# Nystromformer attention and a feed-forward layer on one core: batch 1's second layer by seven products, row variances from ScalarE's sums, W1 loaded into memory of W2 and hT

## The chip, the core and the metric

The kernel runs on one core of a Trainium2 chip. The core has five engines that work side by side and wait for each other by semaphores: TensorE (PE in the profile; PEld are its weight loads), VectorE (DVE), ScalarE (ACT), GpSimd (POOL) and SyncE (SP), and 16 DMA engines. The metric is the time of one execution on the device in microseconds.

## What is computed

Eight batches of eight heads, 576 rows, 64 columns. Attention goes through 32 landmarks (means of 18 rows); the inverse of the landmark matrix comes from six steps of an iteration. Its result is normalized by row, goes through two layers (512 to 2048 to 512) with a ReLU between, and is added to what goes in.

```python
def _attn_ref(q, k, v):
    q_lm, k_lm = q.reshape(B, H, 32, 18, D).mean(axis=3), k.reshape(B, H, 32, 18, D).mean(axis=3)
    A, Bm, C = sm(q, k_lm), sm(q_lm, k_lm), sm(q_lm, k)
    ...
    for _ in range(6):
        Z = 2 * Z - Z @ Bm @ Z
    return A @ Z @ C @ v

def _moe_ref(x, g_ln, w_ch1, w_ch2):
    mu = np.mean(x, axis=-1, keepdims=True)
    var = np.mean((x - mu) ** 2, axis=-1, keepdims=True)
    xn = (x - mu) / np.sqrt(var + 1e-06) * g_ln
    return x + np.maximum(xn @ w_ch1, 0.0) @ w_ch2
```

Inputs and outputs are float32; the kernel multiplies in float16.

## The kernel before

The work is cut into some 1,570 steps ("ops") with names; each step issues a few instructions on one engine. `def_...` functions define them, and the text `ORDER` gives the sequence in which they are issued and the letter of the engine that takes each (P TensorE, D VectorE, A ScalarE, G GpSimd, S SyncE). Each engine executes its own steps in that sequence, so the table is a schedule written out by hand or by a planner; buffers are taken from pools of fixed size (`slots`) at the first use and given back after the last, and a step waits on the chip where it uses a buffer that an earlier step still holds.

The batches go through in a staggered pipeline: while PE does the second layer of one batch, the other engines prepare the attention of the next. The steps by batch `b`:

- `load_...`, `cast_...`: q, k and v come in by DMA. Batch 0's q and k go through `stg` buffers, are cast, and are transposed on PE (`turns`, `turned`) and summed to landmarks (`sums`, tiles `pss_q`, `pss_k`). Of later batches GpSimd's queue loads q and k (`nat_q`, `nat_k`) with a cast on the way.
- `warm_i`: matmuls on zeros (tile `idle`) whose result nobody reads: one block of 24 with 160 columns, and 14 blocks of four with 128.
- `psb`, `softmax`, `gram`, `step`, `next`: the landmark matrix (tile `it`) and the iteration, alternating between PE and DVE; then `zt`, `zc`, `zcbd`.
- `load_w1_i`, `scale_w1_ic` (L346 to L360): W1 comes in eight parts of 512 KB into `w1s` tiles, which share the six `stg` buffers with batch 0's q, k and v, and is scaled by `g` into `w1_16`. `load_w2_i`: W2 comes in four parts on GpSimd's queue, cast to float16 into `w2_16`. `less_mean`, `less`, `center` take the mean out of W1.
- `rows_bi`, `x_bi` (`def_rows`): the attention's result `psy` on PE, and its copy to the row blocks `x_j` of 128 rows. Two batches are nine blocks; four belong to the even batch and five to the odd one (`group_of`).
- `measure_j`, `rstd_b` (`def_measure`): mean and variance of each row by VectorE's BN_STATS and BN_AGGR (L997, L998), and the reciprocal of the deviation on ScalarE (a logarithm and an exponential).
- `psm`, `m16`, `psh`, `relu` (`def_first`): the first layer. Each of 16 `psh` tiles takes four matmuls of 288 columns; its ReLU goes to `hT` on ScalarE or VectorE. `psh` tiles, with several others, share two PSUM buffers (`p2`).
- The second layer. For batches 0 and 1 (`b < FAST`), `pso_...` steps multiply block by block: 16 matmuls of 512 columns each (`def_block`), and one addition on VectorE (`done`). From batch 2 on, the first four blocks go by seven products of half-size matrices instead of eight (`def_seven`): sums and differences of parts of hT (`hmix`: eight a batch) and of W2 (`mix_0` to `mix_3`, once for all batches: 16 steps, `def_mixes`), then 16 matmuls of 256 columns a product (tiles `ps7a`, `ps7e`, `ps7c`), and 14 additions of half a block (`add7`). The odd batch's fifth block stays with `pso`. The very last block is done in two parts, `pso_74a` with 384 columns and `pso_74b` with 128.
- `store_...`: the blocks go out by DMA.

Of the kernel before, what the change touches and what calls it, by code (L numbers as in the profile page):

```python
# [11 lines left out]
UINT32 = mybir.dt.uint32  # L12
AF = mybir.ActivationFunctionType
# [6 lines left out]
0G 20P 23P 4S 12P 14P 24P 17P 11P 2S 1S 3S 6S 7S 10P 21P 28G 38P 25A 26D 34P 39D 40P 29P 30A 31P 27D  # L20
37P 32P 42D 41D 18P 33D 43P 65P 44A 45D 66A 61P 67P 46P 47P 250G 48D 22P 19P 15P 62A 68A 69A 71D
245G 49P 50D 63P 35P 13P 79G 80D 51P 52D 64A 36A 81P 70D 53P 72P 73A 5S 95S 54D 8P 9D 105A 106G 55P
56D 57P 74P 82D 260P 83D 58D 16P 84D 96S 59P 75A 76A 60D 85P 251D 86D 89P 90D 87P 88D 126P 261A 262D
108G 77G 94S 103G 93S 97S 101G 91D 92D 78D 107A 102G 127P 128P 129P 130A 167P 141P 142A 252P 253A
145P 169D 104A 168D 98S 254D 149P 150D 147P 148A 172P 173A 176P 247P 177A 248A 259D 255D 174P 175A
246D 256P 257A 146A 170P 171D 109G 110G 121P 122P 123P 111G 124P 268P 156P 258D 151D 249D 267P 112A
125A 275A 269A 270A 271A 157D 277A 158D 131P 132P 133P 134P 178P 163P 278D 279D 117G 273A 433G 274A
99S 113G 135A 180D 263S 164A 159P 280P 281D 160A 165P 166A 114G 264A 100S 115G 116G 265S 118G 136P
137P 266G 161P 179D 429G 119G 138P 139P 162D 282P 283D 140A 181P 182A 183P 284P 276D 285A 143P 187P
184D 286P 144A 188A 272D 152D 185P 186A 287D 297P 298D 299D 189P 191D 190D 288P 289A 294P 290P 295A  # L30
201P 202P 296A 300P 301A 291D 292P 293A 120G 455G 212P 213P 435G 436G 437G 310P 438G 445G 302A 303G
308P 309A 214P 330P 434D 444D 312D 311D 313D 332D 192P 193A 153D 154D 198P 199A 155A 441D 430D 439D
431D 331D 442D 440D 432D 443D 234P 556D 215P 304P 235P 236P 305A 306A 196P 446G 447G 203P 204P 194P
195A 237P 238P 205P 206P 451G 197A 307G 314P 315A 337P 339P 448G 449D 822G 338A 555D 239P 240P 241P
322P 207P 208P 574D 565D 569G 450D 340A 323A 216P 242D 209D 210S 217P 324D 341P 343D 223P 335P 244S
336A 342D 333P 463D 218P 219P 577G 452D 220D 344P 352P 353D 467G 468G 469G 470G 334A 826G 348P 345A
349A 346P 347A 457G 318P 319A 224P 316P 317A 225P 226P 227P 481P 458G 465D 459G 460G 482A 350P 454D
354D 357P 471D 464D 472D 351A 453D 363P 228P 229P 364D 358A 361P 230P 362A 461D 462D 365D 493P 494A
359P 368P 360A 483P 495P 355P 325D 326D 505A 369A 356A 231D 233A 200G 374P 375P 366P 367A 370P 371A
573G 506D 456D 507P 508P 509D 320P 321D 385P 484P 486A 487A 489A 510P 834D 511D 466D 491A 386P 387P  # L40
485A 388P 211S 512P 376P 473S 474G 490A 377P 496P 498A 501A 499A 497A 513D 514P 327D 488D 492D 328D
396P 397P 475S 476G 566G 828G 829G 830G 831G 572G 477S 478G 838G 839G 844G 564G 568G 503A 378P 379P
380P 515D 823D 502A 221S 504D 372P 516P 479S 480A 500D 517D 836D 528P 529P 530D 531D 398P 399P 373A
381P 522P 518P 389P 329A 866S 382D 418P 519D 824D 559D 520P 521D 523A 532P 419P 420P 524A 533A 534A
558D 550P 551D 552D 553D 548P 549A 421P 422P 423P 536P 424P 425P 848G 535G 832D 833D 554D 232S 867A
537A 538A 539G 560D 525P 527A 400P 401P 557D 426D 427S 605P 526A 606A 840G 841G 594P 595A 561D 540P
541A 390P 391P 611P 612A 837D 596D 827D 392P 393D 825D 850G 851G 852G 563D 603P 604A 853G 562D 859D
842D 860G 861G 843D 579P 613P 614A 407P 580A 601P 602A 609P 610A 1217G 585P 408P 845D 599P 409P 607P
600A 410P 411P 586A 597P 608A 542A 543G 856D 615P 598A 576G 626P 616A 412P 413P 581P 627A 402P 862G
394S 582A 570G 567D 617D 589D 835D 863G 858D 590D 618P 619A 634P 635A 643P 583P 584A 620P 621A 624P  # L50
414P 571G 874P 625A 622P 623A 628P 629A 644P 544P 847D 857D 545A 846D 591D 546A 875D 403P 632P 872S
633A 645P 630P 647P 592D 631A 646P 415D 877P 648P 649P 650P 864D 865D 854D 404D 855D 1191G 886P 638D
637G 641G 663P 664P 665P 639D 640D 662G 428S 417S 406S 661D 593A 882A 884A 879A 880A 883A 652D 878A
651D 657D 887A 889P 892A 896A 658D 666P 668D 894A 895A 849D 667D 653P 654P 711P 722P 712A 723A 891A
890A 655P 656P 547G 575G 675P 676P 677P 728P 729A 678P 695P 696A 1192D 713D 716P 881D 1194D 717A
724P 725A 876P 888P 1213G 660D 587P 870S 714P 416S 659D 871G 873G 384S 1229G 642G 1230G 1231G 726P
898A 715A 679D 682D 669P 897D 727A 588A 730P 222S 1232G 899D 900P 901P 731A 718P 732P 902D 743P 719D
578G 903P 904D 670P 720P 734A 733A 721D 744A 671P 672P 673D 699P 700A 893D 739P 636G 1203D 1239S
# [50 lines left out]
def kernel(  # L109
# [61 lines left out]
    def T(name):  # L171
        return handles[name]
# [1091 lines left out]
```

## Time and profile before

| | us |
|---|---|
| runs before (3), median | 260.66 |
| lowest and highest of them | 260.17, 260.79 |
| span of the profiled execution, first to last instruction | 258.5 |
| PE busy | 249.9 |
| DVE busy | 212.3 |
| POOL busy | 177.5 |
| ACT busy | 163.9 |
| matmuls | 3499 |

The profile is of one execution; its span leaves out what lies around the first and the last instruction, so it stands a little below the runs' times. Rows of the groups show the line of the helper that issued the instruction, the engine, the operation, tile written <- tiles read, shapes, the count, the busy time, the mean time of one in ns, and how long the engine sat idle just before them. L193 issues all matmuls of the steps, so these are told apart by their tiles. A matmul's row begins when it is issued and ends with a modelled end, so neighbours overlap.

### The profile page before, as it was taken

How to read it: one execution, taken by the hardware profiler on the slowest of the kernel's cores; microseconds unless marked ns; L12 is line 12 of the kernel's file. 1: busy time of each engine (PE TensorE's matmuls, PEld its weight loads, DVE VectorE, ACT ScalarE, POOL GpSimd, SP SyncE). 2: the span in 40 equal slices, each digit the busy share in tenths (PEclk: the TensorE clock that was granted, in tenths of full speed). 3: DMA queues.
4: the chain of work that ended last, by engine and by line, in shares of the span. 5: the costliest groups of instructions: out<-in, count | busy, mean ns of one | idle time of the engine just before them, and what ended most of it. 6: DMA issues, size and time to landing. Idle time of an engine off the chain costs nothing.

```text
span 258.5 us, 8351 instructions
## 1 busy us (share of the span) xinstructions
PE 249.9 (97%) x3499; PEld 179.8 (70%) x3499; DVE 212.3 (82%) x472; ACT 163.9 (63%) x304; POOL 177.5 (69%) x180
## 2 busy tenths in 40 slices
PE   7898999999999999999999999999999999999993
PEld 7766465556554557777766787777867787788981
DVE  1669899999999989997998869898547999878661
ACT  1588886747766999778756997868666245644000
POOL 8324899689794789699999995782078505966600
PEclk9999999999999999999999999999999999999999
DMA  6999999999749176949704832500130100510356
GB/s 234 367 269 338 374 210 208 207 235 244 227 127 178 29 164 87 221 89 286 140 4 121 231 93 61 127 3 3 41 85 0 44 20 9 115 23 20 82 121 184
DMA packets 23277, 36.32 MB, mean 140 GB/s; under 512 B 2116, under 2 KB 11592, under 8 KB 23240
## 3 DMA queue, kind: packets, MB, share of 16 engines
q1 hardware_dynamic: 12456, 23.37, 29.6%
q0 software_dynamic: 9504, 10.36, 25.1%
q10 hardware_dynamic: 1280, 2.07, 3.1%
q8 instruction: 27, 0.44, 0.7%
q14 instruction: 10, 0.08, 0.1%
HBM read 36.70 MB, written 9.44 MB: 178 GB/s over the span
## 4 chain that ended last, share of the span: by engine, by line
PE 85%; DMA 7%; ACT 3%; DVE 2%; issue 1%; SPq 1%; ACTq 0%; DVEq 0%
PE psh L193 23%; PE ps7a L193 16%; PE pso L193 15%; PE ps7c L193 8%; DMA w1s<-in_moe_w_ch_dram 5%; PE ps7e L193 4%; PE psm L193 3%; PE psy L193 3%; DMA stg_q<-in_q_dram 3%; PE it L193 2%; PE pscv L193 2%; PE psd L193 1%; PE psec L193 1%; PE psea L193 1%; PE pso_74a L193 1%
## 5 line engine op out<-in xcount | busy, mean ns | idle before, releaser
L203 ACT ACTIVATE hT<-psh 128x576 f16<-128x576 f32 x106 | 65.8, 650 | 30.4 <-PE psh L193 28.6
L193 PEld LDWEIGHTS <-hT 128*128 128x128 f16 x688 | 64.6, 98 | 22.6 <-issue 3.1
L193 PE MATMUL psh<-ea,m 128*128 128x288 f16 x512 | 78.2, 286 | 0.1
L193 PEld LDWEIGHTS <-m 128*128 128x128 f16 x512 | 48.9, 98 | 15.6 <-issue 1.3
L193 PE MATMUL pso<-w,hT 128*128 128x512 f16 x176 | 45.5, 380 | 0.0
L207 POOL TENSOR_TENSOR mix<-hT 128x1024 f16<-128x1024 f16 x8 | 17.0, 2125 | 27.4 <-ACT hT L203 27.4
L210 DVE SCALAR_TENSOR_TENSOR x<-ps7a,rstd,x 128x256 f32<-128x256 f32 x48 | 21.3, 477 | 6.7 <-PE ps7a L193 4.9
L193 PE MATMUL ps7a<-mix,hT 128*128 128x256 f16 x192 | 25.9, 273 | 0.0
L1068 DVE TENSOR_SCALAR hT<-psh 128x576 f16<-128x576 f32 x22 | 16.4, 753 | 10.1 <-PE psh L193 9.9
L997 DVE BATCH_NORM_STATS2 six<-x 128x6 f32<-128x512 f32 x36 | 24.2, 673 | 0.0
L207 POOL TENSOR_TENSOR ea<-ea,lns 128x576 f16<-128x576 f16 (+1 forms) x14 | 17.7, 1261 | 7.2 <-ACT lns L203 4.0
L200 ACT CAST m<-psm 128x512 f16<-128x512 f32 (+1 forms) x25 | 19.1, 793 | 4.5 <-PE psm L193 3.4
L200 ACT COPY x<-psy 128x512 f32<-128x512 f32 (+1 forms) x29 | 16.8, 587 | 7.6 <-PE psy L193 7.2
L193 PEld LDWEIGHTS <-mix 128*128 128x128 f16 x192 | 18.2, 98 | 4.3 <-issue 1.5
L207 POOL TENSOR_TENSOR mix<-mix,hT 128x1024 f16<-128x1024 f16 x8 | 16.9, 2124 | 6.2 <-DVE mix L207 5.8
L207 POOL TENSOR_TENSOR hT<-hT 128x1024 f16<-128x1024 f16 x9 | 19.1, 2123 | 0.2
L207 POOL TENSOR_TENSOR hT<-hT,mix 128x1024 f16<-128x1024 f16 x7 | 15.1, 2166 | 4.4 <-PE ps7e L193 2.5
L214 DVE TENSOR_REDUCE part<-xT_k 128x32 f16<-128x576 f16 x24 | 17.1, 737 | 0.0
L207 POOL TENSOR_TENSOR asum_q<-asum_q 128x256 f32<-128x256 f32 (+1 forms) x24 | 15.1, 628 | 1.5
L203 ACT ACTIVATE ec<-psec 128x256 f16<-128x256 f32 (+1 forms) x42 | 12.4, 428 | 5.3 <-PE psec L193 5.3
L193 PE MATMUL psy<-zcbd,ea 128*128 128x256 f16 x80 | 14.8, 273 | 0.2 <-ACT x L200 0.2
L200 POOL CAST natv<-stg_v 128x1152 f16<-128x1152 f32 (+1 forms) x12 | 13.8, 1163 | 1.4 <-DMA stg_v<-in_v_dram 1.3
(174 smaller groups left out, 471.2 us busy)
## 6 DMA issues: line engine op xcount, KB each, us to landing
out_dram<-x SPq DMA_DIRECT2D x55, 128.0 KB, 2.7
stg_v<-in_v_dram SPq DMA_DIRECT2D x10, 576.0 KB, 5.1
w1s<-in_moe_w_ch_dram SPq DMA_DIRECT2D x8, 512.0 KB, 11.6
nat_q<-in_q_dram POOLq DMA_DIRECT2D x7, 576.0 KB, 8.7
nat_k<-in_k_dram POOLq DMA_DIRECT2D x7, 576.0 KB, 7.5
w<-in_moe_w_ch_dram POOLq DMA_DIRECT2D x4, 512.0 KB, 8.5
out_dram<-x ACTq DMA_DIRECT2D x15, 128.0 KB, 2.4
stg_v<-in_v_dram SPq DMA_DIRECT2D x6, 288.0 KB, 4.5
```

The costliest lines, as they stand in the source:

```text
L193: keep(nc.tensor.matmul(o, l, r, start=start, stop=stop, tile_position=(rb, cb), skip_group_check=(skip or cb != 0)))
L200: keep(nc.scalar.copy(o, i) if e == "A" else ENGINES[e].tensor_copy(out=o, in_=i))
L203: keep(nc.scalar.activation(*args, **kw))
L207: keep(ENGINES[e].tensor_tensor(out=o, in0=a, in1=b, op=f))
L210: keep(ENGINES[e].scalar_tensor_tensor(out=o, in0=a, scalar=s, in1=b, op0=f0, op1=f1))
L214: keep(nc.vector.tensor_reduce(out=o, in_=i, axis=axis, op=f))
L997: keep(nc.vector.bn_stats(out=T(f"six_{j}")[:], in_=T(f"x_{j}")[:]))
L1068: keep(nc.vector.tensor_scalar(out=o, in0=T(psh)[:, :, 0:HS], scalar1=0.0, scalar2=None, op0=ALU.max))
```

## The change

Five edits, and a new `ORDER`:

1. `FAST` goes from 2 to 1: batch 1's first four blocks take the seven products. Its 64 `pso` matmuls and four additions go, and 112 matmuls of 256 columns, eight `hmix` steps and 14 half additions come; the W2 mixes are wanted from batch 1 on.
2. For batches 0 to 2 (`BY_SUMS`) the copy of `psy` to `x` also gives the row's sum. The variance then comes from one ScalarE instruction, a Square of (sum - 512 x) with its sum over the row, in place of BN_STATS and BN_AGGR. In the list all 13 measures of these batches go to ScalarE; Of the 14 copies with a sum 11 stand on ScalarE and three on VectorE, there as a TENSOR_SCALAR.
3. W1's parts 0 to 3 are loaded into the memory of `w2_16` and parts 4 to 7 into that of batch 1's `hT`, so that they need no `stg` buffer; W2's loads and batch 1's hT then wait until those parts are scaled.
4. Pools: `s16` has three buffers where it had four.
5. The list: five relus go from VectorE to ScalarE, five W2 mixes and one hT mix more stand on VectorE, seven hT mixes more and five W2 mixes fewer on GpSimd, besides smaller exchanges.

```diff
 ORDER = """
-0G 20P 23P 4S 12P 14P 24P 17P 11P 2S 1S 3S 6S 7S 10P 21P 28G 38P 25A 26D 34P 39D 40P 29P 30A 31P 27D
...
+0G 15P 17P 13P 22P 12P 19P 16P 11P 14P 21P 2S 26A 18P 20P 23P 250G 24P 32P 33A 1S 34P 25D 29P 31P
...
-    FAST = 2
+    FAST = 1
+    BY_SUMS = (0, 1, 2)
...
+    def copy_summed(e, o, i, total):
+        if e == "A":
+            act(o, i, AF.Copy, accum_out=total)
+        else:
+            keep(nc.vector.tensor_scalar(out=o, in0=i, scalar1=1.0, scalar2=0.0, op0=ALU.mult, op1=ALU.add,
+                                         accum_out=total))
...
-                    ("part", 2), ("tot", 3), ("lmt", 4), ("s16", 4), ("sT", 1),
+                    ("part", 2), ("tot", 3), ("lmt", 4), ("s16", 3), ("sT", 1),
...
+        def place_of(i):
+            f, half = divmod(i, 2)
+            if f < 2:
+                return w2_16[:, ts(i, 4), :].rearrange("p m d -> p (m d)").bitcast(FP32).rearrange(
+                    "p (c d) -> p c d", c=2)
+            return T(hT(1))[:].rearrange("p m t -> p (m t)")[:, ts(i - 4, 4 * DM)].bitcast(FP32).rearrange(
+                "p (c d) -> p c d", c=2)
...
-            n = f"w1s_{i}"
-            buf(n, "stg", [P, 2, DM], FP32)
             f, half = divmod(i, 2)
-            op(f"load_w1_{i}", "S", (n,),
-               lambda e, n=n, f=f, half=half: dma(
-                   e, T(n)[:], w1_src[:, 2 * half:2 * half + 2, ts(f, DM)]))
+            op(f"load_w1_{i}", "S", held(i),
+               lambda e, i=i, f=f, half=half: dma(e, place_of(i), w1_src[:, 2 * half:2 * half + 2, ts(f, DM)]))
...
+                st, six = T(f"stats_{b}")[:, u, :], T(f"six_{j}")
+                if e == "A":
+                    act(squares[:], T(f"x_{j}")[:], AF.Square, bias=st[:, 0:1], scale=-float(DM), accum_out=st[:, 1:2])
+                    return
...
-            act(T(f"lnv_{b}")[:, 0:n], T(f"stats_{b}")[:, 0:n, 1], AF.Ln, bias=eps_ln[:], scale=UP * UP)
+            act(T(f"lnv_{b}")[:, 0:n], T(f"stats_{b}")[:, 0:n, 1], AF.Ln, bias=eps_ln[:],
+                scale=UP * UP / DM ** 3 if summed else UP * UP)
```

How the list moves instructions, at three places.

TensorE's queue at the start (`idle` are the blocks on zeros, here the one of 24 with 160 columns; `pst_k`, `pst_q` are batch 0's transposes, `pss_k`, `pss_q` its sums), before:

```order
L193 MATMUL idle_247<-zeros_63 128x160
L193 LDWEIGHTS zeros_63
L193 MATMUL idle_272<-zeros_63 128x128
...
L193 MATMUL idle_272<-zeros_63 128x128
L197 LDWEIGHTS nat_k_277
L197 MATMUL pst_k_279<-ident16_64,nat_k_277 128x128
```

and now:

```order
L196 MATMUL pss_q_313<-pm16_67,nat_q_301 128x64
L196 LDWEIGHTS zeros_63
L196 MATMUL idle_323<-zeros_63 128x160
...
L196 MATMUL idle_323<-zeros_63 128x160
L196 LDWEIGHTS nat_k_253
L196 MATMUL pss_k_291<-pm16_67,nat_k_253 128x64
```

The block of 24, which was the eighth block of all, stands behind the first sums of q and ahead of k's second sums and transposes; all 14 blocks of four stand ahead of the first transposes, where six stood behind them. On SyncE's queue all eight parts of W1 now stand ahead of batch 1's v, where one stood behind half of it, in the order 2, 3, 0, 5, 1, 4, 6, 7 (before 2, 3, 1, 0, 4, 5, 6, 7).

ScalarE's queue between the exponentials of batches 2 and 3 (`ec`, from `psec`) and batch 1's deviation (`lnv`), before:

```order
L203 ACTIVATE ec_1782<-psec_1747 128x2x2x32
L203 ACTIVATE ec_1782<-psec_1747 128x4x2x32
L200 CAST natv1_77<-stg_v_1878 128x2x9x64
L203 ACTIVATE hT_1334<-psh_1857 128x576
L203 ACTIVATE lnv_2026<-stats_1368,eps_ln_73 128x5
```

and now (`squares` is written by a Square and read by nobody; its sum goes to `stats`):

```order
L206 ACTIVATE squares_75,stats_731<-x_1542,stats_731 128x512
L206 ACTIVATE x_1774,stats_731<-psy_1614 128x512
L206 ACTIVATE ec_1716<-psec_1679 128x4x2x32
L206 ACTIVATE hT_743<-psh_1765 128x576
L206 ACTIVATE ec_1716<-psec_1679 128x4x2x32
L203 CAST natv1_78<-stg_v_1734 128x2x9x64
L206 ACTIVATE squares_75,stats_731<-x_1533,stats_731 128x512
L206 ACTIVATE squares_75,stats_731<-x_1774,stats_731 128x512
L206 ACTIVATE lnv_1934<-stats_731,eps_ln_73 128x5
```

Three Squares and a copy with a sum have come in among the exponentials and the last relu of batch 1.

VectorE's queue at the very end (the last block's two parts, and ahead of them the last half additions), before:

```order
L210 SCALAR_TENSOR_TENSOR x_4938<-ps7c_5378,rstd_5299,x_4938 128x256
L210 SCALAR_TENSOR_TENSOR x_5211<-ps7a_5219,rstd_5299,x_5211 128x256
L210 SCALAR_TENSOR_TENSOR x_5206<-ps7a_5219,rstd_5299,x_5206 128x256
L210 SCALAR_TENSOR_TENSOR x_5267<-pso_74b_5394,rstd_5299,x_5267 128x128
L210 SCALAR_TENSOR_TENSOR x_5267<-pso_74a_5497,rstd_5299,x_5267 128x384
```

and now:

```order
L220 SCALAR_TENSOR_TENSOR x_5158<-ps7c_5414,rstd_5392,x_5158 128x256
L220 SCALAR_TENSOR_TENSOR x_5368<-ps7a_5383,rstd_5392,x_5368 128x256
L220 SCALAR_TENSOR_TENSOR x_5262<-ps7a_5383,rstd_5392,x_5262 128x256
L220 SCALAR_TENSOR_TENSOR x_5095<-pso_74a_5459,rstd_5392,x_5095 128x384
L220 SCALAR_TENSOR_TENSOR x_5095<-pso_74b_5543,rstd_5392,x_5095 128x128
```

The two parts have changed places, on PE as on VectorE: the 16 matmuls of the small part are now PE's last.

210 lines of the change are left out of this document (115 added, 95 removed).

## The prediction

> **What bounds the kernel now.** I read the busy shares first, then the windows, then the chain of work that ended last, and last the groups that the change touches.
>
> ```profile
> span 258.5 us, 8351 instructions
> PE 249.9 (97%) x3499; PEld 179.8 (70%) x3499; DVE 212.3 (82%) x472; ACT 163.9 (63%) x304; POOL 177.5 (69%) x180
> PE 85%; DMA 7%; ACT 3%; DVE 2%; issue 1%; SPq 1%; ACTq 0%; DVEq 0%
> ```
>
> TensorE is busy for 97% of the span, and 85% of the chain lies on it; the 7% on DMAs is the start. A busy PE need not be at its peak, so I look at how fast it goes where it carries the chain (start us, length us, what).
>
> ```profile
> 52.08 1.73 PE pso L193 x8
> 98.61 0.98 PE psh L193 x8
> 245.87 1.75 PE ps7a L193 x16
> ```
>
> A product of 512 columns takes 1.73 / 8 = 0.216 us, one of 288 columns 0.1225, one of 256 columns 1.75 / 16 = 0.109: time goes with the columns, from 52 us to 246 us alike. So between the start and the end a product that is left out is time saved, as long as the others come no later. The windows say where that holds (stretch, length, then PE, PEld, DVE, ACT, POOL busy, clock, DMA share, GB/s).
>
> ```profile
> 0.00:10.00 10.00, 8.16 (x101) 7.99 (x101) 3.18 (x11) 2.60 (x3) 6.29 (x29) 1.00 0.80 292
> 10.00:20.00 10.00, 8.70 (x247) 6.58 (x245) 7.17 (x25) 8.13 (x14) 2.85 (x4) 1.00 1.11 286
> 20.00:30.00 10.00, 9.35 (x127) 5.59 (x126) 8.93 (x22) 7.94 (x21) 6.66 (x10) 1.00 1.07 365
> 30.00:40.00 10.00, 9.67 (x145) 6.21 (x145) 9.63 (x26) 8.20 (x17) 9.18 (x13) 1.00 1.19 240
> 50.00:60.00 10.00, 10.00 (x73) 5.46 (x72) 9.95 (x20) 5.83 (x11) 7.74 (x10) 1.00 1.13 248
> 90.00:100.00 10.00, 10.00 (x82) 6.35 (x81) 9.08 (x18) 9.51 (x17) 9.06 (x12) 1.00 0.74 145
> ```
>
> From 40 us on PE has no free time that a window shows, while VectorE is nearly as full up to 130 us. Before 40 us PE is free for 1.30 + 0.65 + 0.33 = 2.3 us of the last three of these first windows, and the DMA engines are full (shares over 1). The chain says what PE waits for there, and what comes at the end:
>
> ```profile
> 15.84 11.95 DMA w1s<-in_moe_w_ch_dram
> 27.81 0.73 ACT w L203
> 252.53 1.64 PE pso_74a L193 x10
> 254.19 0.62 DVE x L210
> ```
>
> **Term 1, batch 1's second layer: -1.6 us.** Four of batch 1's five blocks go from 16 products of 512 columns each (64) to seven half-size products of 16 matmuls of 256 columns each (112). Removed: 64 x 0.216 = 13.84 us. Added: 112 x 0.109375 = 12.25 us. All of it stands on PE between about 60 and 90 us, where PE is full, so the difference counts whole: -1.59 us. Two waits come with it. The products wait for the four mixes of W2, which are wanted a batch earlier, and for eight mixes of hT; behind a waiting product the whole of PE's queue stands still. I take 0, since two of the seven products need no mix and stand first, and name a late mix as the price: up to 2.1 us, once.
>
> **Term 2, the end: -0.3 us.** The last block is stored in two parts. Before, PE ends with the part of 384 columns, whose addition takes 0.62 us; now it ends with the part of 128 columns (0.35 us), and the larger addition runs beside the small part's 16 matmuls.
>
> ```profile
> 252.57 0.35 DVE L210 SCALAR_TENSOR_TENSOR x<-pso_74b,rstd,x 128x128 f32<-128x128 f32 x1 [0.43 <-PE pso_74b L193]
> out_dram<-x SPq DMA_DIRECT2D x1, 96.0 KB, 2.1
> out_dram<-x ACTq DMA_DIRECT2D x1, 96.0 KB, 2.4
> out_dram<-x SPq DMA_DIRECT2D x2, 32.0 KB, 2.7
> ```
>
> That is 0.35 - 0.62 = -0.27 us. The last store is then 32 KB where it was 96 KB; the landings (2.1 to 2.7 us) don't order by size, so I count nothing for it; by these rows it lies between -0.3 and +0.6 us.
>
> **Term 3, the other engines: 0 us.** These are the groups (busy us, mean ns of one):
>
> ```profile
> L997 DVE BATCH_NORM_STATS2 six<-x 128x6 f32<-128x512 f32 x36 | 24.2, 673 | 0.0
> L998 DVE BATCH_NORM_AGGREGATE stats<-six 128x2 f32<-128x6 f32 x36 | 6.6, 182 | 1.2
> L210 DVE SCALAR_TENSOR_TENSOR x<-ps7a,rstd,x 128x256 f32<-128x256 f32 x48 | 21.3, 477 | 6.7 <-PE ps7a L193 4.9 <-ACT rstd L203 0.9 <-PE psh L193 0.6
> L210 DVE SCALAR_TENSOR_TENSOR x<-pso,rstd,x 128x512 f32<-128x512 f32 x11 | 8.0, 731 | 0.4 <-PE pso L193 0.4
> L203 ACT ACTIVATE w<-w1s,g_sb 128x512 f16<-128x512 f32 x4 | 2.9, 720 | 0.9 <-DMA w1s<-in_moe_w_ch_dram 0.9
> L200 ACT COPY x<-psy 128x512 f32<-128x512 f32 x24 | 13.9, 588 | 6.7 <-PE psy L193 6.4
> L207 POOL TENSOR_TENSOR hT<-hT 128x1024 f16<-128x1024 f16 x9 | 19.1, 2123 | 0.2
> L207 POOL TENSOR_TENSOR mix<-w 128x512 f16<-128x512 f16 x5 | 5.8, 1156 | 0.0
> L207 DVE TENSOR_TENSOR mix<-w 128x512 f16<-128x512 f16 x3 | 1.3, 452 | 0.0
> L203 ACT ACTIVATE hT<-psh 128x576 f16<-128x576 f32 x106 | 65.8, 650 | 30.4 <-PE psh L193 28.6 <-DVE mix L207 0.8
> L1068 DVE TENSOR_SCALAR hT<-psh 128x576 f16<-128x576 f32 x22 | 16.4, 753 | 10.1 <-PE psh L193 9.9
> ```
>
> VectorE loses 13 measures (13 x 0.855 = 11.1 us), four whole additions (2.9) and five relus (3.8); it gains 14 half additions (6.7), five mixes of W2 (2.3) and a mix of hT (0.8): about -8 us. ScalarE gains 13 Squares and five relus (3.3). No row shows a Square; the nearest is the scaling of W1, 128x512 from SBUF with an operand per partition, at 0.72 us: 9.4 us, +13 us in all. The sums that it now gives beside copies and Squares have no row; I bound them by nothing and by the 0.13 us that the scaling stands above the plain copy (24 or so times, 3 us), and take nothing. GpSimd gains seven mixes of hT (14.9) and loses five of W2 (5.8): +9 us. So DVE would stand at 204, ACT at 177, POOL at 187 of some 257 us. A Square also waits for its row's sum, which mostly ScalarE itself has just given. All three engines stay below PE, so this work is hidden; if that cover failed, one Square is 0.72 us and one mix 2.1 us of waiting.
>
> **Term 4, the start: 0 us, between -2.3 and +1.6 us.** W1 no longer waits for `stg` buffers, but the DMA engines are full from 10 to 40 us, and the bytes ahead of W1's sixth part (k, q, v, five parts) are the same; what PE waits for at 27.8 us therefore lands when it did. GpSimd's two loads of batch 1's q and k, which share the DMA engines with W1, move too, q's ahead of a cast and k's behind one; their bytes are the same, and I count 0. If W1 came earlier, PE could win its free time there, 2.3 us. Against that, the block of 24 idle matmuls is moved from ahead of the first transposes to behind the first half's sums. Twelve idle matmuls of 128 columns end in 0.84 us (below), so 24 of 160 columns take 24 x 0.07 to 0.09 us = 1.7 to 2.1 us, and k's and q's second halves queue behind them: sums that started at 10.24 us start at up to 11.8, so up to +1.6 us for the iteration of batch 0. That delay ends in the wait for W1, which I take to hide it. W2's loads now wait until W1's first four parts are scaled out of its memory, and GpSimd's scalings of the last parts and loads of the next q and k are queued behind them; they stood behind those scalings on GpSimd's queue already, and the DMA engines are full for long after (share 1.13 in 50 to 60 us): 0, at most one scaling, 0.7 us.
>
> ```profile
> 1.40 6.26 PE L193 MATMUL idle<-zeros 128*128 128x128 f16 x56 [1.40 <-DVE zeros L252]
> 10.24 0.44 PE L193 MATMUL pss_q<-pm,nat_q 128*128 128x64 f16 x9 [0.18 <-DVE nat_q L200]
> 13.11 0.84 PE L193 MATMUL idle<-zeros 128*128 128x128 f16 x12
> ```
>
> **Sum.** -1.59 - 0.27 = -1.86 us: the profiled execution's span goes from 258.5 to 256.6 us. That span lies 2.2 us below the median of the runs shown, 260.66 us, and I leave that distance as it is: **258.8 us**.
>
> **Rivals.**
>
> *The start gets shorter too* (0.20). For it: W1's eight loads are issued at once and all ahead of batch 1's v, and the list is new where PE is free. Against it: DMA shares over 1. PE's 2.3 us go: 256.5 us.
>
> *The start gives it back* (0.17). The delay of the iteration isn't hidden by W1. For it: step follows step there, each behind the one before. It costs 1.0 to 1.6 us, say 1.3: 260.1 us, no change.
>
> *ScalarE makes PE wait* (0.08), which ends slower. A `psh` bank of PSUM comes free when its relu is done, and there are two. ScalarE works in order, so a Square ahead of a relu holds PE's next `psh` by up to 0.72 us. The place is batch 1's and 2's measures, beside the exponentials of the next set: in 90 to 100 us ScalarE has only 0.5 us free already. It decides from four fully exposed Squares of the 13 ((1.86 + 0.78) / 0.72 = 3.7); with seven it is 258.8 + 5.0 = 263.8 us. Against it: ScalarE waits for `psh` for 28.6 us in all, so it is mostly early.
>
> *PE's clock falls in the start* (0.05). The six blocks of four idle matmuls that stood behind the first transposes now stand ahead of them. The first 56 idle matmuls take 6.26 us, 112 ns each, though the later twelve take 70 with their tail; so PE is slow at first, whatever the clock column says. If it fell back for as long again, half of 6.26 us would be lost: 261.9 us. Against it: 8.7 of 10 us busy in that window. [...]
>
> [...] First the rows:
>
> ```profile
> L207 DVE TENSOR_TENSOR w<-w,less 128x1024 f16<-128x1024 f16 x8 | 6.4, 816 | 0.0
> 85.66 1.54 DVE L207 TENSOR_TENSOR w<-w,less 128x1024 f16<-128x1024 f16 x1
> ```
>
> The usual one of these eight takes 0.68 us, one took 1.54 beside an instruction of GpSimd. Six more such instructions at the mean excess of 0.13 us add 0.8 us to VectorE. [...]
>
> **Chances and range.** Forecast 0.50 (258.0 to 259.6), and the rivals as above. A measurement tells about 0.3%, 0.78 us, from no change: below 259.88 us is faster, above 261.44 slower. The forecast and the first rival are faster (0.70), the second is the same (0.17), and the third and the fourth are slower (0.13). The range reaches from the first rival's full gain to beyond the second, 256.4 to 260.9 us; about 0.18 is left out, mostly above.
>
> **What would show it.** 3547 matmuls and PE busy about 248 us at the pitches above (term 1); an addition of 0.35 us as the last (term 2); DVE about 204, ACT about 177 with Squares near 0.72 us, POOL about 187 (term 3); the scaling of W1's sixth part near 27.8 us and PE full from 40 us (term 4). The prediction is wrong if the windows after 40 us show PE below 10.0, or relus that wait behind Squares while PE waits for `psh`.

## The result: slower, and the profile after

| | before | after |
|---|---|---|
| time, median (runs) | 260.42 us (4) | 263.30 us (4) |
| lowest, highest | 260.17, 260.79 | 262.66, 264.06 |
| span of the profiled execution | 258.5 | 261.5 |

The ratio is 1.0115, with a 95% interval from 1.0088 to 1.0143: the change costs 2.9 us, where 1.9 us were to be won. Ratios here and below leave disturbed executions out, medians don't. The page of the kernel after: its span, the engines' busy time, and the shares of the chain of work that ended last.

```profile
span 261.5 us, 8490 instructions
PE 250.4 (96%) x3547; PEld 185.3 (71%) x3547; DVE 205.7 (79%) x457; ACT 177.0 (68%) x352; POOL 183.1 (70%) x179
PE 75%; DMA 8%; DVE 8%; ACT 3%; issue 2%; POOL 1%; DVEq 0%; ACTq 0%; POOLq 0%
```

VectorE and ScalarE ended where they were forecast (204 and 177), GpSimd a little below (187). But PE carries 75% of the chain instead of 85%, and VectorE 8% instead of 2%: PE waits more. The windows say where (stretch, length, then PE, PEld, DVE, ACT, POOL busy, granted clock, DMA share, GB/s).

```profile
10.00:20.00 10.00, 8.33 (x204) 6.39 (x201) 5.33 (x17) 6.64 (x13) 2.58 (x3) 0.86 1.11 318
20.00:30.00 10.00, 9.44 (x137) 5.45 (x130) 8.77 (x24) 7.99 (x21) 7.35 (x11) 0.97 1.08 355
70.00:80.00 10.00, 8.98 (x294) 6.78 (x294) 8.97 (x25) 6.93 (x20) 9.98 (x8) 1.00 0.70 172
240.00:250.00 10.00, 8.68 (x79) 7.39 (x78) 8.54 (x16) 1.16 (x3) 4.24 (x2) 1.00 0.45 120
```

Three places stand out: the start, where the clock fell to 0.86 for one window (its records show half speed from 17.2 us, for 3.41 us), 70 to 80 us, and 240 to 250 us; in the last two before had PE full. The fall of the clock belongs to single executions: the four of after, at 264.06, 263.93, 262.66 and 262.66 us, had mean clocks of 0.990, 1.000, 0.998 and 0.990, and 3.41 us at half speed alone take 0.0065 off that mean. So the second and the third had no such stretch, and were no faster for it. Busy time hides small pauses, so I also summed over all matmuls by how much the distance from one start to the next exceeds 0.417 ns a column and 3 ns (0.216 us for 512 columns and 0.109 for 256, by the pitches of the chain's rows); each excess counts where it begins, and the time to the first matmul counts too. This lost time of PE, in us (tail and v40e are experiments below):

```
            0-40   40-70   70-90   90-240   240-end   sum
before      12.0     1.7     1.8     7.3       0       22.9
after       12.7     2.5     3.4     7.3       1.5     27.4
tail        11.8     2.6     3.1     7.7       0       25.3
v40e        11.9     2.4     2.3     7.2       0       23.8
```

After loses 4.5 us more and works some 1.5 us less; that is the 3.0 us by which the spans differ. Of the 4.5 us, 0.7 are lost up to 40 us, 0.8 from 40 to 70, 1.6 from 70 to 90, and 1.5 at the end. The places one by one. At the start, the chain now begins with GpSimd's load of batch 1's q (start us, length us, what):

```profile
4.66 12.54 DMA nat_q<-in_q_dram
17.23 1.12 PE psl_q L196 x9
```

The sum of batch 1's q (`psl_q`) stands on PE in the middle of batch 0's iteration and waits 0.6 us for that load. At 78 us PE stops inside a step of set 2's iteration (timeline of PE: start, length, what, and in brackets the idle time ahead of it):

```profile
78.17 0.23 PE L196 MATMUL it<-st 32*32 32x64 f16 x7 [0.28 <-DVE st L220]
79.14 0.23 PE L196 MATMUL it<-st 32*32 32x64 f16 x7 [0.74 <-issue]
```

Seven matmuls of one step, then nothing for 0.93 us from start to start, then the next seven; "issue" says that PE waited for nothing that the profile shows. And at the end, on VectorE, GpSimd and PE:

```profile
243.83 2.59 DVE L217 TENSOR_TENSOR mix<-mix,hT 128x1024 f16<-128x1024 f16 x1
```

```profile
243.76 2.12 POOL L217 TENSOR_TENSOR hT<-hT 128x1024 f16<-128x1024 f16 x1
```

```profile
246.48 1.05 PE L196 MATMUL ps7a<-mix 128*128 128x256 f16 x8 [1.32 <-DVE mix L217]
```

A mix of batch 7's hT took 2.59 us on VectorE, where such a mix takes 0.68. GpSimd had begun one 0.07 us earlier; PE's next product waits 1.32 us. Last, groups that term 3 and term 2 spoke of (busy us, mean ns of one):

```profile
L206 ACT ACTIVATE squares<-x,stats 128x512 uint8<-128x512 f32 x13 | 9.6, 736 | 0.1
L206 ACT ACTIVATION_READ_ACCUMULATOR squares<-x,stats 128x1 f32 x13 | 2.7, 208 | 0.0
L1033 DVE BATCH_NORM_STATS2 six<-x 128x6 f32<-128x512 f32 x23 | 15.7, 680 | 1.6 <-ACT x L203 1.6
L220 DVE SCALAR_TENSOR_TENSOR x<-pso_74b,rstd,x 128x128 f32<-128x128 f32 x1 | 0.4, 351 | 0.3 <-PE pso_74b L196 0.3
```

### The profile page after: what moved, and what is told of

Its sections match the earlier page's. It is cut to its first block, busy times and chain, and to the rows that moved or that the text cites. A ratio compares the mean times of both kernels' runs of the same rounds, so it can differ in the third digit from the quotient of the medians.

```text
span 261.5 us, 8490 instructions
## 1 busy us (share of the span) xinstructions
PE 250.4 (96%) x3547; PEld 185.3 (71%) x3547; DVE 205.7 (79%) x457; ACT 177.0 (68%) x352; POOL 183.1 (70%) x179
## 4 chain that ended last, share of the span: by engine, by line
PE 75%; DMA 8%; DVE 8%; ACT 3%; issue 2%; POOL 1%; DVEq 0%; ACTq 0%; POOLq 0%
PE psh L196 21%; PE ps7a L196 18%; PE ps7c L196 8%; PE pso L196 6%; DMA nat_q<-in_q_dram 5%; PE ps7e L196 4%; PE psm L196 3%; PE psy L196 3%; DMA stg_v<-in_v_dram 3%; PE it L196 2%; PE psec L196 2%; DVE mix L217 2%; DVE x L220 1%; PE pscv L196 1%; PE psd L196 1%
## 5 line engine op out<-in xcount | busy, mean ns | idle before, releaser
L206 ACT ACTIVATE hT<-psh 128x576 f16<-128x576 f32 x111 | 68.8, 653 | 29.4 <-PE psh L196 28.8
L220 DVE SCALAR_TENSOR_TENSOR x<-ps7a,rstd,x 128x256 f32<-128x256 f32 x56 | 25.5, 477 | 13.9 <-PE ps7a L196 12.4
L196 PE MATMUL ps7a<-mix,hT 128*128 128x256 f16 x224 | 29.4, 273 | 0.0
L217 POOL TENSOR_TENSOR mix<-mix,hT 128x1024 f16<-128x1024 f16 x11 | 23.7, 2160 | 7.7 <-DVE mix L217 7.4
L196 PE MATMUL pso<-w,hT 128*128 128x512 f16 x112 | 28.6, 379 | 0.0
L217 POOL TENSOR_TENSOR hT<-hT 128x1024 f16<-128x1024 f16 x11 | 23.3, 2125 | 0.2
L1108 DVE TENSOR_SCALAR hT<-psh 128x576 f16<-128x576 f32 x17 | 12.7, 748 | 6.5 <-PE psh L196 6.4
L1033 DVE BATCH_NORM_STATS2 six<-x 128x6 f32<-128x512 f32 x23 | 15.7, 680 | 1.6 <-ACT x L203 1.6
L196 PE MATMUL ps7a<-mix 128*128 128x256 f16 x112 | 15.2, 273 | 1.3 <-DVE mix L217 1.3
L203 POOL CAST natv<-stg_v 128x1152 f16<-128x1152 f32 (+1 forms) x11 | 12.7, 1161 | 5.1 <-DMA stg_v<-in_v_dram 5.0
L196 PE MATMUL ps7a<-w,hT 128*128 128x256 f16 x112 | 15.7, 273 | 0.0
```

The source lines that it names most:

```text
L196: keep(nc.tensor.matmul(o, l, r, start=start, stop=stop, tile_position=(rb, cb), skip_group_check=(skip or cb != 0)))
L203: keep(nc.scalar.copy(o, i) if e == "A" else ENGINES[e].tensor_copy(out=o, in_=i))
L206: keep(nc.scalar.activation(*args, **kw))
L217: keep(ENGINES[e].tensor_tensor(out=o, in0=a, in1=b, op=f))
L220: keep(ENGINES[e].scalar_tensor_tensor(out=o, in0=a, scalar=s, in1=b, op0=f0, op1=f1))
L1033: keep(nc.vector.bn_stats(out=six[:], in_=T(f"x_{j}")[:]))
```

## The experiments

The theory: PE works as much less as forecast, and loses more than that at three separate places. The rivals: the change's parts themselves cost it (sums, W1's memory, the seven products), or the places share one bound. Fifteen kernels were run; each time stands beside runs of before on the same chip (260.3 to 260.6 us). The edits are in the list but for three kernels; lines of diffs give engine and step.

### Idle matmuls as before (warm)

```diff
-P warm_0 (the block of 24) behind sums_q0, six blocks of four ahead of the first transposes
+P warm_0 ahead of turns_k0; warm_8, 12, 9, 5, 3, 6 between the products and steps of the iteration
```

> The changed kernel with its blocks of idle matmuls where they stood before: the block of 24 ahead of the first transposes, the six blocks of four between the products and steps of batch 0's iteration. Nothing else moves. Theory (the clock): PE's half-speed window of 3.41 us at 17.2 to 20.6 us comes from the idle matmuls that no longer fill the gaps; the clock stays at 1.0 from 10 to 30 us and up to half of 3.41 us comes back: 261.6 to 262.3 us against 263.3. Rival (PE waits there anyway): the window goes, and the time stays at 263.3 +- 0.4, since what PE waits for (batch 1's q, W1, the normalizing) comes no earlier.

Measured: 262.61 us, ratio 1.0079 (1.0055 to 1.0103). The windows of warm:

```profile
10.00:20.00 10.00, 9.43 (x245) 6.96 (x243) 6.40 (x22) 7.99 (x14) 4.11 (x6) 1.00 1.11 311
20.00:30.00 10.00, 8.98 (x127) 5.05 (x125) 8.79 (x20) 7.69 (x25) 6.23 (x10) 1.00 1.08 360
```

The clock stays at 1.00, PE gets through 245 matmuls where it had 204, and 0.7 us come back: less than the theory's 1.0 to 1.7, more than the rival's 0.4. The interval overlaps that of after, so the size is rough, and it isn't shown that the clock is the reason. In the kernel tail, next, the idle matmuls stand where the change has them, and the clock of its profiled execution stays at 1.00 all the same, with less of PE busy (window of tail):

```profile
10.00:20.00 10.00, 7.84 (x220) 5.58 (x217) 5.98 (x22) 7.20 (x14) 3.99 (x6) 1.00 1.11 304
```

### The tail's mix on VectorE (tail)

```diff
 D hmix_714
+D hmix_724
-G hmix_724 (behind hmix_704)
```

> The changed kernel with one mix of batch 7's hT (third mix, second half) on VectorE, right behind the mix that took 2.60 us at 243.83 us, instead of on GpSimd. Theory (a shared port): that mix took 2.60 us and not 0.70 because GpSimd's mix, issued 0.07 us earlier, held it; with GpSimd's mix gone it takes 0.7 us, PE's gap of 1.49 us before the next half-size product goes, and the time falls by 1.3 to 1.5 us: 261.8 to 262.0 against 263.3. Rival (the mix waits for something else, such as the sum that GpSimd made last): the long mix stays, or the gap reappears a few products later since the moved mix is now VectorE's: 263.0 to 263.3.

Measured: 261.61 us, ratio 1.0042 (1.0025 to 1.0059), 1.7 us less than after. VectorE and PE of tail at that place:

```profile
243.28 0.68 DVE L217 TENSOR_TENSOR mix<-mix,hT 128x1024 f16<-128x1024 f16 x1
243.88 0.69 DVE L217 TENSOR_TENSOR hT<-hT 128x1024 f16<-128x1024 f16 x1
```

```profile
243.57 1.91 PE L196 MATMUL ps7a<-mix 128*128 128x256 f16 x16
```

Both mixes take 0.7 us on VectorE, and PE runs through. Without GpSimd's mix beside it the first one isn't held; and it runs ahead of the other here, so it had not been waiting for the other's result. In after it ended at 246.42 us, 0.54 us behind the end of GpSimd's at 245.88; so 2.05 of its 2.59 us were spent beside the other, and in tail it takes 0.68. That a port is what the two share, as the theory has it, no trace shows.

### The list of before for the first 60 us (start60), and batch 1 by whole products (fast2)

```diff
-the first 60 us in the list of after
+the first 372 entries of the list of before, then the rest as after
```

> The changed kernel with the list of before for the first 372 entries (about 60 us: batch 0's preparation, set 1's, W1, the first half of the first layer), on the same engines as before but for the copies of rows and the measures of variance, which stay where the change has them; W1's memory, the sums and batch 1's seven products stay as changed. Theory (the new list of the start and of 40 to 60 us costs PE its time): PE's idle time summed by the starts of its products rose by 2.0 us up to 60 us, so 261.3 us, and the chain no longer begins with a 12.5 us load of batch 1's q nor has a load of v of 8 us at 39 us. Rival (W1's memory or the Squares cost it, not the list): 263.3 +- 0.5.

```diff
-    FAST = 1
+    FAST = 2
-P 28 seven_1..., D add7_1..., hmix_1...
+P 32 pso_10 to pso_13 at their places, D done_10 to done_13
```

> The changed kernel with batch 1's first four blocks by whole products again (64 of 512 columns instead of 112 of 256), spread over the places of the seven half-size products in the list; no mixes of hT for batch 1; all else as changed. Theory (the half-size products save what was predicted, and the loss lies elsewhere): 1.6 us slower than the changed kernel, 264.9. Rival (the mixes and half additions of batch 1 on VectorE delay the steps of set 2's iteration, 1.34 us of gaps at 77 to 79 us, and eat the gain): 263.2 to 263.7, with no gap ahead of the steps at 77 to 79 us.

Both missed by far: 271.32 us, ratio 1.0424 (1.0388 to 1.0461), and 270.66 us, ratio 1.0380 (1.0333 to 1.0426). PE's waits of start60 from 60 to 70 us and what VectorE does ahead of them, then PE's waits of fast2 (waiter <- what ended it: total, times, longest):

```profile
PE psp L196 <- DVE m L220: 5.0, 1, 5.0
```

```profile
59.73 4.89 DVE L217 TENSOR_TENSOR mix<-w 128x512 f16<-128x512 f16 x3
```

```profile
PE psea L195 <- issue: 1.9, 1, 1.9
PE pso L195 <- DMA w<-in_moe_w_ch_dram: 1.9, 1, 1.9
PE psp L195 <- DVE part L223: 1.8, 1, 1.8
```

Two lists that don't fit each other, or steps put evenly into another's places, bring waits of their own: in start60 a mix of W2 on VectorE took 3.44 us beside three instructions of GpSimd that came one after the other. Neither run says what its part costs in a list made for it; term 1 was not isolated. They do show the same two kinds of wait again, VectorE's mixes held beside GpSimd's work (4.89 us for three) and "issue" (1.9 us).

### The sum of q later (q11), two loads later (loads), VectorE's variances (nosums), four moves together (all1)

All four contain tail's edit, so 261.6 us is their base.

```diff
-P total_q11 between step_0_2 and step_0_3
+P total_q11 ahead of total_q10
```

> The kernel with the tail's mix moved (261.6 us), and batch 1's first sum of q (total_q11, which waits on PE for GpSimd's load of q) moved on PE from between the third and fourth step of batch 0's iteration to ahead of total_q10, behind the fifth step. Theory (a wait on a load stands on PE's queue in the middle of the iteration): the gap of 1.1 us ahead of psl_q at 15.5 us goes and what follows comes earlier: 260.5 to 261.0 us. Rival (W1 or the rows' sums bound the next 20 us anyway): the gap moves to the second steps or to psf and psy, 261.4 to 261.8 us.

```diff
-G load_k40, S load_v40 among the steps of set 2
+G load_k40, S load_v40 behind step_2_5
```

> The kernel with the tail's mix moved (261.6 us), and the loads of batch 4's k (GpSimd's queue) and v (SyncE's queue) moved in the list from among the fourth and fifth step of set 2's iteration to behind its sixth. Theory (PE runs out of instructions: its instructions come in 16 KB packets through the same DMA engines, and a packet that waits behind bulk loads comes late; PE goes on 1.4 us after it has landed): the packet that starts at 75.8 us starts 1 to 2 us earlier, the stall of 0.83 us inside the fourth step and the one ahead of it (0.35) go: 260.4 to 260.9 us. Rival 1 (small matmuls use instructions up faster than any packet comes): the packet and the stall stay, 261.6 +- 0.3. Rival 2 (loads that come later are waited for later): the gain is given back at batch 4's preparation, 261.5 or more.

```diff
-    BY_SUMS = (0, 1, 2)
+    BY_SUMS = ()
-A measure_0 to measure_12
+D measure_0 to measure_12
```

> The kernel with the tail's mix moved (261.6 us), but the rows' variance of batches 0 to 2 from VectorE's two instructions again (13 measures of 0.855 us) instead of ScalarE's sums and Squares, at the same places of the list. Theory (the sums are hidden and cost PE nothing, but VectorE has no room left up to 130 us): VectorE near 216 us, ScalarE near 161, and PE waits longer for additions and mixes at 50 to 100 us: 262.5 to 265 us. Rival (ScalarE's Squares and its separate reads of the accumulator, 24 at about 0.2 us, hold PE up at 50 to 60 us): 260.5 to 261.3 us.

> Four moves in the list at once, all of the change's parts kept: the tail's mix, the idle matmuls as before, batch 1's sum of q later, the two loads of batch 4 later. Theory (these four places are where the gain went): the parts add up, 261.6 - 0.7 (clock, as measured by the idle matmuls alone) - 0.8 (load of q) - 1.0 (instructions) = 259.1 us, between 258.6 and 259.8, below the 260.4 of before. Rival (they share one bound in the first 45 us, the loads of W1 and W2): 260.2 to 261.0 us.

Measured: q11 263.92 us, ratio 1.0141 (1.0101 to 1.0181); loads 261.61, ratio 1.0047 (1.0025 to 1.0070); nosums ratio 1.0489 (some 273 us; the runs lie apart, 272.2 to 277.3); all1 263.20, ratio 1.0084 (1.0054 to 1.0115).

q11 missed. Its PE waits no longer for the load, but W1's scaling and the steps are waited for instead, and at 123 us a new wait has come, in all1 too (PE's waits, q11 and then all1):

```profile
PE psy L196 <- ACT x L203: 1.7, 1, 1.7
```

```profile
PE psy L196 <- ACT x L203: 2.0, 1, 2.0
```

There ScalarE's copy of batch 3's rows waits for memory that the store of batch 0's first block still holds; that wait differs from run to run, so I don't put q11's loss down to it alone. In q11's profiled execution the clock also stands at half speed for 3.41 us, from 22.5 us, and its four executions have mean clocks of 0.980 to 0.994. The loads' move changed nothing, but tells little: SyncE has only loads and stores, so by my reading it issued the v load as soon as its memory was free, wherever it stood in the list. And nosums answers for the sums: with the measures back on VectorE (218.3 us busy) the kernel is some 11.6 us slower than tail by the ratios, far above the 262.5 to 265 us expected, so the ScalarE sums are no burden but what this list lives on. What they are worth in a list made without them it doesn't say, and its profiled execution (277.25 us) has 13.7 us at half clock.

```profile
PE 255.3 (93%) x3547; PEld 186.4 (68%) x3547; DVE 218.3 (79%) x481; ACT 168.0 (61%) x315; POOL 181.2 (66%) x178
PE 56%; DVE 23%; POOL 9%; issue 4%; DMA 4%; ACT 2%; ACTq 0%; POOLq 0%; DVEq 0%
```

### Three moves (fix3), and fewer idle matmuls on top (phase)

```diff
 tail's and warm's edits, and
-A store_0_1 (near 119 us)
+S store_0_1 behind store_2_0
```

> The changed kernel with three moves in its list: the tail's mix on VectorE, the idle matmuls as before, and the store of batch 0's first block's second half (store_0_1), which stands on ScalarE's queue near 119 us, put on SyncE's queue some 220 entries earlier; a copy of batch 3's rows waits for its memory, by 0 to 2 us from run to run. Batch 1's sum of q and the loads stay where the change has them. Theory (three separate causes, each on PE's path): 261.6 - 0.7 - 0.5 = 260.4 us, between 259.8 and 260.9, no gap ahead of the rows of batch 3 near 123 us, and single runs closer together than the tail's move alone (260.4 to 262.4). Rival (the waits share a bound, as the four moves together seemed to): 261.3 us or more.

```diff
-        warm(4, 128)
+        warm(2, 256)
```

> The changed kernel, list untouched, with each of its 14 blocks of four idle matmuls of 128 columns as two of 256 columns (the same columns, 28 matmuls fewer ahead of everything else). Theory (PE runs out of instructions at a place set by how many it has been given since the start): the packet that started at matmul 1102 and the stall of 0.9 us inside the fourth step of set 2's iteration move 28 matmuls further in the program, out of that step into the products of ea behind it, and what was 0.93 us is at most 0.6: 262.6 to 263.3 us. Rival (the step waits for something of its own, a result or a buffer): the stall stays inside the fourth step with 0.7 to 0.9 us, 263.3.

Unlike its expectation says, phase was run on the list of fix3, so it is compared with fix3. Measured: fix3 261.36 us, ratio 1.0026 (1.0004 to 1.0048); phase 261.23, ratio 1.0018 (0.9995 to 1.0040). fix3 missed its 260.4: the waits at the end and at 123 us are gone, but PE, which comes sooner to the second layer, waits there for W2, as it did for 0.6 us in tail's and warm's profiles; behind that wait, from 41.9 us, the clock of its profiled execution (262.45 us) stands at half speed for 3.41 us.

```profile
PE pso L196 <- DMA w<-in_moe_w_ch_dram: 1.7, 1, 1.7
```

The pause at "issue", first in fix3, then in phase (timelines of PE):

```profile
78.86 0.23 PE L196 MATMUL it<-st 32*32 32x64 f16 x7 [0.18 <-DVE st L220]
79.85 0.24 PE L196 MATMUL it<-st 32*32 32x64 f16 x8 [0.75 <-issue]
```

```profile
77.84 0.42 PE L196 MATMUL psea<-xT_q,lm 32*32 32x288 f16 x15
78.91 0.44 PE L196 MATMUL psea<-xT_q,lm 32*32 32x288 f16 x13 [0.64 <-issue]
```

With 28 matmuls fewer at the start it has left the step and stands in the products of `ea` behind it. Counted through, it comes after the 1118th matmul in both, as in every kernel that has it. Its size was expected to fall to 0.6 us and stayed at 0.93. So it is tied to how many instructions PE has been given, not to what they are. The DMA view of the page shows what comes in such portions:

```profile
q8 instruction: 27, 0.44, 0.7%
```

27 packets of 16 KB (0.44 MB / 27) for 3547 matmuls and as many weight loads: one packet for 131 of each on average. The trace has each packet's start and landing, but not when it is asked for; my estimate for that, from this average, is PE's 990th matmul, 128 ahead of the pause. Its times, and those of the pause itself (us):

```
          990th mm   packet starts   lands    last mm before   PE goes on   pause
after       74.02        76.73       77.69        78.21          79.14       0.93
warm        72.63        74.88       75.76        76.72          77.39       0.67
tail        73.22        75.78       76.71        77.31          78.14       0.83
fix3        74.82        77.63       78.56        78.91          79.85       0.94
phase       74.72        76.72       77.68        77.98          78.91       0.93
fast2       76.66        80.20       81.18        80.31          82.53       2.22
```

In all of them PE goes on 1.2 to 1.6 us after the packet has landed, and the packet starts 2.0 to 3.5 us after the 990th matmul. How many instructions PE holds ahead, no trace shows.

### What holds the packet up (v40), and W2 sooner (w2q, best)

Why does it start so late? DMA shares of after around it (last columns: clock, DMA share, GB/s):

```profile
73.00:74.00 1.00, 1.00 (x24) 0.68 (x23) 0.96 (x4) 1.00 (x5) 1.00 (x2) 1.00 0.00 0
74.00:75.00 1.00, 1.00 (x25) 0.68 (x24) 1.00 (x4) 1.00 (x3) 1.00 (x2) 1.00 0.61 108
75.00:76.00 1.00, 1.00 (x79) 1.00 (x72) 1.00 (x3) 1.00 (x3) 1.00 (x2) 1.00 0.99 311
76.00:77.00 1.00, 1.00 (x42) 0.73 (x31) 0.97 (x3) 0.94 (x5) 0.98 (x2) 1.00 1.24 351
```

Loads of v begin just as the 990th matmul is reached, and in the third of these microseconds PE uses up 79 matmuls. So three kernels, all with fix3's moves; in v40 ScalarE issues the load, at a place of its own program, since SyncE can't be held back by the list.

```diff
-S load_v40 (v40, best)
+A load_v40 behind eas_11
-G load_w2_0, load_q20, load_w2_1, load_w2_2 (w2q, best)
+G load_w2_0, load_w2_1, load_w2_2, load_q20
```

> The kernel with three moves (fix3, 261.4 us), and the load of batch 4's v issued by ScalarE at a place of its program near 82 us instead of by SyncE, where it went out as soon as its memory was free (a move in the list alone doesn't delay SyncE, which has only loads and stores: the two loads moved before didn't thin out the traffic of 76 to 79 us). Theory (PE runs out of instructions at its 1118th matmul, since the packet asked for some 128 matmuls earlier waits 2.6 to 2.8 us behind that bulk, and PE goes on 1.3 to 1.6 us after its landing): the packet starts within 1.5 us of matmul 989, and the stall of 0.94 us falls below 0.3 us: 260.3 to 260.8 us. Rival (the packet comes 2.5 us late whatever the bulk does): the stall stays at 0.7 to 0.9 us, 261.4.

> The kernel with three moves (fix3: tail's mix, idle matmuls, store; 261.4 us), and on GpSimd's queue W2's second and third quarter ahead of the load of batch 2's q instead of behind it. Theory (what the start wins ends in a wait for W2: pso waits 1.7 us for a load of W2 at 40.2 us in that profile): the wait at 40 us goes or falls below 0.5 us and the time falls by 0.8 to 1.6 us: 259.8 to 260.6 us. Rival 1 (the second layer's first block is not what the later work waits for): the gap goes and another of the same length comes by 60 us, 261.4 +- 0.4. Rival 2 (batch 2's q is then late): a new wait of GpSimd's sums near 45 us reaches PE, above 261.8 us.

> The kernel with three moves (fix3, 261.4 us), W2's second and third quarter ahead of batch 2's q, and batch 4's v issued by ScalarE: every part of the change is kept. Theory (three waits of the order, W2 and the instructions, each on PE's path, took the gain): 261.4 - 1.0 - 0.8 = 259.6 us, between 258.8 and 260.2, faster than before by about 0.3%. Rival (the order of the start, with W1 in W2's memory, gives back whatever is won): 260.6 us or more.

Measured: v40 260.62 us, ratio 1.0003 (0.9987 to 1.0019); w2q 267.25, ratio 1.0239 (1.0200 to 1.0279); best 267.08, ratio 1.0236 (1.0199 to 1.0274). The load went out at 78.1 us in v40. Its DMA view of 73 to 74 us, its windows with the DMA share, and PE at the place of the pause:

```profile
q8 instruction: 1, 0.02, 6.5%
```

```profile
73.00:74.00 1.00, 1.00 (x24) 0.70 (x22) 1.00 (x4) 1.00 (x3) 1.00 (x2) 1.00 0.07 16
74.00:75.00 1.00, 1.00 (x81) 0.98 (x71) 1.00 (x3) 1.00 (x3) 1.00 (x2) 1.00 0.00 0
```

```profile
77.10 0.26 PE L196 MATMUL it<-st 32*32 32x64 f16 x11 [0.19 <-DVE st L220]
77.23 0.58 PE L196 MATMUL psea<-xT_q,lm 32*32 32x288 f16 x28
```

The packet starts 0.55 us after the 990th matmul (73.05) and lands at 74.64; PE passes the 1118th without a pause. So do best, cast and v40e, where ScalarE issues that load too; w2q, where SyncE issues it, has a pause of 1.16 us there. By all this I read the pause as PE running out of instructions, because the packet waited behind bulk loads. With it gone, 0.7 us are back (the intervals of fix3 and v40 overlap, so the size is rough).

w2q met its rival 2, and best the same wait. The wait for W2 is gone, and batch 2's q, now behind it on GpSimd's queue, is waited for instead (row of w2q):

```profile
PE pszc L196 <- DVE st L506: 5.9, 1, 5.9
```

In best it is 6.4 us, and in both the clock then stands at half speed for 6.83 us, from some 47.5 us. So W2 and batch 2's q, which share GpSimd's queue while the DMA engines move 200 GB/s in all (w2q, 30 to 40 us), are both due; in these lists neither could go ahead of the other for nothing.

### Mending what v40 made late (cast, v40e)

In v40 ScalarE's cast of batch 4's v waits 1.62 us for the later load, and PE 0.6 us behind that.

```diff
-A cast_v40 ahead of eas_12
+A cast_v40 behind m16_201
```

> The kernel with the three moves and batch 4's v issued by ScalarE (v40, 260.6 us), and the cast of that v on ScalarE put behind the exponentials and copies that stood behind it: in v40's profile it waits 1.62 us at 85.5 us for the load that now starts later, and PE waits 0.6 us for the exponentials behind it. Theory (a wait at the head of an in-order queue): ScalarE's wait and PE's 0.76 us gap ahead of psm at 86.4 us go: 259.8 to 260.2 us, faster than before by 0.1 to 0.2%. Rival (batch 2's first layer waits for something else there): 260.6 +- 0.3.

```diff
-A load_v40 behind eas_11
+A load_v40 behind rstd_1
```

> The kernel with the three moves, and batch 4's v issued by ScalarE behind batch 1's rstd (some 1.5 us sooner than in v40, where it went out at 78.1 us, landed 7.3 us later and was waited for by ScalarE for 1.6 us at 83.9 us). Theory (the load lands by 84 us, and the packet of instructions asked for at 73 us has gone ahead of it): no stall at the 1118th matmul, no wait of the cast, PE's gap of 0.76 us ahead of psm at 86.4 us below 0.3: 259.8 to 260.2 us. Rival (bulk that starts sooner holds the packet up again, or another wait takes the gap's place, as behind the moved cast): 260.5 us or more.

Measured: cast 261.28 us, ratio 1.0037 (1.0025 to 1.0049), a miss: the cast now holds a logarithm that PE waits for. v40e 260.42 us, ratio 0.9991 (0.9971 to 1.0010): the same as before. Its span, and its longest waits of PE from 20 to 130 us:

```profile
span 257.9 us, 8488 instructions
```

```profile
PE psf L196 <- POOL w L378: 0.9, 2, 0.6
PE pso L196 <- DMA w<-in_moe_w_ch_dram: 0.4, 1, 0.4
```

Every part of the change is in it; only places in the list differ. It takes 2.9 us less than after and ties with the kernel before; no version here beats that one.

## Why the prediction was wrong

**Term 1, work: right; "so the difference counts whole" and the 0 for its waits: wrong.** Lost time taken off the spans, PE works 258.5 - 22.9 = 235.6 us before and 257.9 - 23.8 = 234.1 in v40e, 1.5 us less, where terms 1 and 2 together were 1.86. PE's busy time, 248 us by forecast, is 247.9 in tail and 247.7 in v40e (250.4 in after's execution with the stretch at half speed). What failed is the step that counted nothing beside this work. What feeds PE with instructions was not in my sum: the pause of 0.93 us, and its undoing in v40 by a load issued later, point to it. It need not come from the half-size products, for fast2, without them, has one of 2.22 us; in the new list PE uses up the 128 matmuls ahead of it in 4.2 us, as bulk loads start, where before took 5.9 us and had its packet 0.6 us after the 990th matmul. "A late mix: up to 2.1 us, once" had the right price and the wrong batch: batch 7's cost 1.5 us.

**The waits beside GpSimd, priced by their mean.** I counted six more such instructions of VectorE at the mean excess of 0.13 us. Rare the long ones were: of 74 TENSOR_TENSOR instructions of VectorE in after, three stood above their usual time by more than 0.15 us. But the mean says nothing of where the one long wait falls. At 244 us there is no other batch left whose work PE could do meanwhile, so the whole of it was on the path: 1.7 us by the run, the largest single piece.

**Term 2, the end: right.** The last addition takes 0.351 us.

**Term 3, other engines: right, ScalarE in part by luck.** VectorE 205.7, ScalarE 177.0, Squares 736 ns. The sums' price, which I took as nothing, is an instruction of its own of some 0.2 us, 24 times, some 5 us in all; ScalarE's total agrees only because other work there shrank by about as much. After's waits of PE for `psh` come to 0.2 us, so the rival with ScalarE did not come about.

**Term 4, the start at 0: near in size; its clock rival came in some executions.** Up to 40 us PE loses 12.0 us before, 12.7 in after's profiled execution, with the clock at half speed for 3.41 us, and 11.8 in tail's, with the same idle matmuls and the clock at 1.00. The rival with the clock, at 0.05, is thus, by the mean clocks, what two of four executions of after show, but they took no longer than the other two, and what it is worth stays open. PE was not idle ahead of the fall: in the 3.41 us before it (13.78 to 17.20 us) it was busy for 2.30 us. My argument against the rival, 8.7 of 10 us busy, was taken from before, whose idle matmuls filled the pauses. And "W2's loads wait: 0, at most one scaling": PE's wait for W2 was 0.4 to 1.7 us in the profiles of mended lists, so that part of what the start wins ends there.

**The sum.** Forecast 258.8, measured 263.3: 4.5 us. The tail's mix gave 1.7 back, the idle matmuls and the store another 0.25 on top of it (the idle matmuls alone 0.7; both within overlapping intervals), the packet of instructions 0.9 with v40e: 260.4. Of the other 1.6 us, v40e's span shows 1.3 (257.9 against 256.6; its twelve executions span 257.7 to 259.3): 0.9 of lost time above before's and 0.4 of work less saved than counted. By the table the 0.9 lies between 40 and 90 us, not in the start: 0.56 us ahead of the first `pso` at 41.0 us, where W2 is waited for, and 0.35 us ahead of a step at 76.6 us, where VectorE's `st` is. What would take them away was not found.

## What to carry to other kernels

Where many small matmuls follow each other, count instructions as well as columns, and look whether bulk loads start where the next packet of instructions is due (here one for 131 matmuls on average): the pause of 0.93 us that the profile put down to "issue", and that kept its number in PE's sequence, the 1118th matmul, was gone when a load came later. Price a wait by whether other work can take its place, not by how often it happens: the one held mix at the end was paid whole (1.7 us by the run). In mid-kernel such a wait can be paid too, as in start60, where PE waited 5.0 us behind the held mixes. Look at the granted clock of every execution before a fall of the clock in one profile is called the cause: here the executions without it were no faster.

## What the runs showed of the hardware

- The profile counts instruction packets among the transfers of the DMA engines (27 of 16 KB in after). Where the DMA share was low (0.07 from 73 to 74 us in v40 and in before), a packet started 0.5 us after the 990th matmul (v40, v40e; 0.6 in before); behind bulk loads, 2.0 to 3.5 us (phase, fast2). There PE went on 1.2 to 1.6 us after the landing (phase, warm).
- A mix of W2 on VectorE took 3.44 us beside three GpSimd instructions that came one after the other (start60), where such a mix took 0.42 in after.
- A sum given beside a ScalarE instruction is read by an instruction of its own: 208 ns after a Square, 13 times, and 207 after a copy, nine times (after).
- The changes of the granted clock lay 10.24, 3.413 and 238.93 us apart in after, which is 3, 1 and 70 times 3.413; a stretch at half speed lasted 3.41 us (after, q11, fix3) or 6.83 (w2q, best). In the 3.41 us ahead of it PE was busy for 2.30 us (after), 2.10 (q11), 1.83 (fix3) or 0 (w2q, best); but a stretch in phase with PE busy for 1.93 us (40.0 to 43.4 us) was not followed by a fall, so no threshold comes out of these traces.
